# A causal FFT convolution on one core: spectrum products by 64x64 and 64x32 tiles, with the sums moved into the inverse transform

## The chip, the cores and the metric

The kernel runs on one core of a Trainium2 chip. The metric is the time of one execution on the device in microseconds (us). TensorE multiplies matrices, VectorE (DVE), ScalarE (ACT) and GpSimd (POOL) work elementwise, SyncE (SP) issues most transfers. TensorE's weights stay in its 128x128 array while the other operand streams past; a matmul can use a part of the array, a tile, given by its rows (the partitions it sums over) and columns (the partitions it writes).

## The reference

Everything is float32, S = 2048 tokens, D = 640 channels, F = 1728.

```
mod = silu(c) @ w_mod                        # six rows: sa, ca, ga, sb, cb, gb
h  = layernorm(q) * (1 + ca) + sa
ks = shift_conv(k, shift_k, 4 taps)          # causal, per channel
kv = ks * v
y  = irfft(rfft(kv, 2S) * rfft(ssm_k, 2S))[:S] + kv * ssm_D
x  = q + ga * (h * y)                        # a causal convolution of length S per channel
h2 = layernorm(x) * (1 + cb) + sb
out = x + gb * (W2 gelu(W1 layernorm(h2)^T + b1) + b2)^T      # the token-mixing MLP
```

## The kernel before

The convolution runs in five chunks of 128 channels (`for c in range(NC)`), then come the second layernorm, the first MLP product (L432) and the second (L1026 and L951). The order of instructions on each engine is the order of the code, so a chunk's stages stand one behind the other on TensorE, and the work of other engines is dealt out between them by hand (`dv(n)` issues the next n operations of the shift convolution).

A chunk's transform of 2048 tokens is split into 64 x 32. Both sides, the signal kv (in tile `x`) and the SSM kernel (permuted by `perm` on ScalarE into tile `p`), go through

- `step1` (L210), step one: a transform over 64 points for the 128 channels; two halves of 64 channels share the partitions, and the constant F1 has zeros for the other half. A matmul has 64 columns of data as weights (a 128x64 tile) and streams 128 columns. ScalarE copies the result to tile `z`.
- `f2` (L224), step two: for each of 64 frequencies k1 a 32-point transform. The constant `w2` (4 MB, tiles `w0` and `w1`) holds 128x64 weights, half of them zeros; 64 columns stream. Eight frequencies fill one PSUM buffer. Real and imaginary parts lie beside each other in a row of memory. ScalarE copies the SSM side to `kt`; VectorE multiplies the signal side with it and with its swapped copy (`mul`, two products into `p`); GpSimd forms real part minus and imaginary part plus (`add`, two sums into `y`).
- `i2` (L255), step three: the inverse over 32 points, data as weights on 32x128 tiles, real and imaginary part accumulated in PSUM.
- `i1` (L273), step four: the inverse over 64 points on 64x64 tiles; then `gate` multiplies by h and adds to x.

PSUM has a ring of three buffers for all of this. `load_ks(c + 2)` fetches the SSM kernel two chunks ahead into `aux`, from which `perm` has to read before. In the last chunk the first blocks of W1 are split into two float32r parts (`split_rows`, into `wb`), which the first MLP product uses.

Of the kernel before, what the change touches and what calls it, by code (L numbers as in the profile page):

```python
# [20 lines left out]
def _constants():  # L21


    n1, n2, k1, k2 = np.arange(64), np.arange(32), np.arange(64), np.arange(32)
# [6 lines left out]
    w2 = np.zeros((2, 32, 2, 64, 2, 2, 32))  # L31
    for c in range(2):
        w2[0, :, c, :, 0, c] = np.cos(ang)
        w2[1, :, c, :, 0, c] = -np.sin(ang)
        w2[0, :, c, :, 1, c] = np.sin(ang)
        w2[1, :, c, :, 1, c] = np.cos(ang)
    ang = 2 * np.pi * (k2[:, None] * n2[None, :] % 32) / 32
    c, s = np.cos(ang), np.sin(ang)
    v2 = np.tile(np.concatenate([c, -s, s, c], 1), (4, 1))
# [5 lines left out]
    return {"small": small.astype(np.float32), "w2": w2.reshape(128, 8192).astype(np.float32),  # L45
# [4 lines left out]
def mixer_kernel(ctx: ExitStack, tc: tile.TileContext, q, k, v, shift_k, ssm_k, ssm_D, w1, b1, w2, b2, c,  # L50
# [29 lines left out]
    T_z, T_y, T_v1 = mem("z", 8192), mem("y", 4096), mem("v", 4520)  # L80
    T_w2 = [mem("w0", 4096), mem("w1", 4096)]
# [7 lines left out]
    KSP = P.rearrange("p (i m) -> p i m", i=32)  # L89
# [7 lines left out]
    Y = T_y.rearrange("p (r i k) -> p r i k", r=2, i=32)  # L97
    W2 = [t.rearrange("p (k m) -> p k m", m=64) for t in T_w2]
# [64 lines left out]
    def perm(c):  # L163
        act.activation(KSP.rearrange("p i (n e) -> p i e n", e=2),
                       KSR.rearrange("p (e i n) -> p i e n", e=2, i=32), AF.Copy)

# [5 lines left out]
    def kv_ops(g, eng=dve):  # L172
# [8 lines left out]
        ops.append(lambda: TT(eng, X.rearrange("p (n i) -> p n i", i=64)[:, 8 * g:8 * g + 8], S_,  # L181
# [13 lines left out]
    def kv(c_next, gs=((0,), (1,), (2,), (3,))):  # L195

        ops = []
        for gl in gs:
            o = kv_ops(gl[0])

            def end(gl=gl, last=o.pop()):
                last()
                if c_next is not None:
                    for g in gl:
                        kv_loads(c_next, g)
            ops += o + [end]
        return ops


    def step1(side, t, later=False):  # L210

        ps = psum()
        for a in range(8):
            i = 8 * t + a
            lhs = KSP[:, i] if side else X.rearrange("p (m i) -> p i m", i=32)[:, i]
            o = 512 * (a % 2) + 128 * (a // 2)
            for ri in range(2):
                pe.matmul(ps[64 * ri:64 * ri + 64, o:o + 128], lhs, F1[:, 128 * ri:128 * ri + 128], start=True,  # L218
                          stop=True)
# [4 lines left out]
    def f2(g):  # L224

        ps = psum()
        for kk in range(8):
            k1 = 8 * g + kk
            for ri in range(2):
                for h in range(2):  # L230
                    o = 128 * kk + 64 * ri
                    rhs = bass.AP(tensor=T_z.tensor, offset=T_z.offset + 128 * h + 2 * k1,
                                  ap=[T_z.ap[0], [256, 32], [1, 2]])
                    pe.matmul(ps[64 * h:64 * h + 64, o:o + 64], W2[k1 // 32][:, 2 * (k1 % 32) + ri], rhs, start=True, stop=True)  # L234
        pv = ps.rearrange("p (m s i) -> p m s i", s=2, i=32)
        xs_ = pv[:, :, 0]
        kt = KT[g % 2]
        act.activation(kt.rearrange("p (m i) -> p m i", i=32), pv[:, :, 1], AF.Copy)  # L238
        pa, pb = P[:, 1024 * (g % 2):1024 * (g % 2) + 512], P[:, 1024 * (g % 2) + 512:1024 * (g % 2) + 1024]
        m16 = lambda t: t.rearrange("p (m i) -> p m i", i=32)  # L240
# [225 lines left out]
    run(kv_ops(2, pool))  # L466
    run(kv_ops(0))
    kv_loads(1, 0)
    run(kv_ops(1))
    kv_loads(1, 1)  # L470
    kv_loads(1, 2)
    run(kv_ops(3))
    sync.dma_start(T_w2[0], c_w2[:, 0:4096], max_dma_last_dim=4096)
    kv_loads(1, 3)
    sync.dma_start(T_w2[1], c_w2[:, 4096:8192], max_dma_last_dim=4096)
# [6 lines left out]
    perm(0)  # L482
    all_taps()
    load_taps(2)
    for t in range(4):
        step1(0, t)
    run(kv_ops(2, pool))
    run(kv_ops(0))
    run(kv_ops(1))
    for t in range(4):  # L490
        step1(1, t)
# [12 lines left out]
    fill = kv_ops(3)  # L504
# [6 lines left out]
    for c in range(NC):  # L511
        cn = c + 1 if c + 1 < NC else None
        ac, po = a1_ops(c)
        pend_m = pend_a = None
        for g in range(8):
            m_, a_ = f2(g)
            if pend_m:
                pend_m()
            if pend_a:
                pend_a()  # L520
            pend_a, pend_m = (pend_m and pa_next), m_
            pa_next = a_
            if c:
                for f_ in ac[2 * g:2 * g + 2]:
                    f_()
            if cn is None and g < 4:

                act.activation(X[:, 512 * g:512 * g + 1], epsc, AF.Copy)
                for b in range(2):
                    sync.dma_start(X[64 * b:64 * b + 64, 512 * g:512 * g + 512],  # L530
                                   dram(w1, (16 * b + g) * F, [[32 * F, 64], [1, 512]]))
            dv(-(-len(fill) // max((6 if c else 8) - g, 1)))
            if c and cn is not None and g == 3:
                perm_add(cn)
        pend_m()
        if pend_a:
            pend_a()
        pa_next(dve if c else pool)
# [5 lines left out]
        if c and c + 2 < NC:  # L544
            taps()
            if c + 3 < NC:
                load_taps(c + 3)
        if c == 0:
            mod_load(0, 4, P[:, 0:1920])
            for t in range(4):  # L550
                step1(0, t)
# [26 lines left out]
            run(kv_ops(2, pool))  # L578
# [5 lines left out]
            perm(1)  # L584
            load_ks(2)
            run(ac[8:16])
            run(po[0:2])
            fill.extend(kv(3, ((0,), (1, 2), (3,))))
        elif cn is not None:
            for t in range(2):  # L590
                step1(0, t)
            perm(cn)
            if c + 2 < NC:
                fill.extend(kv(c + 3 if c + 3 < NC else None))
            else:
                fill.extend(x1s(cc, j) for cc in range(c) for j in range(16))
        else:
            blk.update({f: (j16(t[:, 0:2048]), j16(t[:, 2048:4096])) for f, t in (
                (0, mem("w0", 4096, "wb0")), (1, mem("w1", 4096, "wb1")))})
# [6 lines left out]
            split_rows(0, X, (0, 1, 3))  # L606
            split_rows(1, T_aux[:, 0:2048], (0, 1, 3))
            run(po)
        if c:
            dv(7 if cn is not None else 8)  # L610
            i2(0)
            if cn is None:
                mod_part(tap, 3, pl[3])
                i2(1, dve)
                t = mem("y", 4096, "wb2")
                blk[2] = j16(t[:, 0:2048]), j16(t[:, 2048:4096])
                split_rows(0, X, (2,))
                split_rows(1, T_aux[:, 0:2048], (2,))
# [466 lines left out]
```

## Time and profile before

| | |
|---|---|
| time, median of 3 runs (lowest to highest) | 721.0 us (720.58 to 728.29) |
| the profiled execution | 722.7 us, of it a span of 720.8 us from first to last instruction |
| TensorE busy, weight loads busy | 91%, 88% of the span |
| VectorE, ScalarE, GpSimd busy | 68%, 41%, 21% |
| chunk stages; MLP | about 23 to 315 us; 315 to 721 us |
| step two in the five chunks | 42 to 67, 117 to 137, 168 to 187, 218 to 237, 269 to 288 us |

A group's row gives line, engine, operation, output and inputs by the program's names, shape and count, then busy time, the mean of one in ns, and the idle time of the engine ahead of it with what ended most of that. Names are those of tiles: `pst` is any buffer of the PSUM ring, `tap` the PSUM tile of the taps, `z` the spectrum before step two or four, `y` the product spectrum, `v` the constants, `x`, `p`, `kt`, `aux` as above. The clock in a view is the share of full speed that was granted to TensorE. The MATMUL records of a float32 matmul number two for each matmul of the program.

### The profile page before, as it was taken

To read this page: it belongs to the slowest core of one execution; us is meant where nothing else is said; L and a number is where in the kernel's file an instruction comes from. 1 tells how busy PE (TensorE), PEld (TensorE's weight loads), DVE (VectorE), ACT (ScalarE), POOL (GpSimd) and SP (SyncE) were. 2 spreads that over 40 slices of the span, in tenths; PEclk is the share of its full clock that TensorE was granted. 3 is DMA by queue.
4 is the path that set the end of the run, shared out by engine and by line. 5 is a ranking of instruction groups with operands and counts; after the bars stand their busy time and mean duration, and the time that the engine had idled before them with its cause. 6 is when DMAs were issued, how large, how long until landed. Compare 5 with 4: busy or idle time off the path is not lost.

```text
span 720.8 us, 20751 instructions
## 1 busy us (share of the span) xinstructions
PE 656.0 (91%) x9131; PEld 632.6 (88%) x9131; DVE 492.6 (68%) x861; ACT 297.4 (41%) x465; POOL 154.6 (21%) x135
## 2 busy tenths in 40 slices
PE   0797968999999999998889999999999989999997
PEld 0797758989999989777889999999999989999997
DVE  7666748969879638788894313212389768888887
ACT  0432564645745545446766223112244222333221
POOL 5187038715626328100010000000000000000000
PEclk9998889999999899879999999999999999999999
DMA  9979998527233522351203543352263423455510
GB/s 185 243 223 223 304 235 172 116 52 164 57 68 87 168 55 70 112 133 44 53 7 59 101 75 60 76 100 59 59 183 102 141 96 123 130 159 175 159 45 37
DMA packets 165903, 84.89 MB, mean 118 GB/s; under 512 B 88979, under 2 KB 157366, under 8 KB 165814
## 3 DMA queue, kind: packets, MB, share of 16 engines
q1 hardware_dynamic: 161266, 82.27, 46.1%
q10 hardware_dynamic: 4548, 1.31, 1.0%
q8 instruction: 71, 1.16, 0.7%
q14 instruction: 18, 0.15, 0.1%
HBM read 73.07 MB, written 10.49 MB: 116 GB/s over the span
## 4 chain that ended last, share of the span: by engine, by line
PE 54%; DVE 23%; ACT 6%; issue 5%; POOL 5%; DMA 4%; SPq 2%; ACTq 0%; DVEq 0%; POOLq 0%
PE pst L432 21%; PE pst L218 8%; PE pst L234 8%; PE pst L1026 7%; PE pst L263 5%; DVE m_w L59 4%; POOL y L59 4%; DVE m_x L59 3%; PE pst L282 3%; DVE tap L59 2%; ACT m_w L939 2%; PE pst L951 2%; DVE kt L59 2%; DVE m_x L960 1%; DVE m_v L59 1%
## 5 line engine op out<-in xcount | busy, mean ns | idle before, releaser
L234 PE MATMUL pst<-z,w 128*64 128x64 f32 x2560 | 96.8, 241 | 11.2 <-ACT z L220 6.1
L234 PEld LDWEIGHTS pst<-z,w 128*64 128x64 f32 x2560 | 95.4, 142 | 12.9 <-ACT z L220 7.3
L59 POOL TENSOR_TENSOR y<-p 128x256 f32<-128x256 f32 x72 | 90.6, 1315 | 27.2 <-DVE p L59 26.7
L59 DVE TENSOR_TENSOR p<-pst,kt 128x512 f32<-128x512 f32 x80 | 52.7, 688 | 29.6 <-ACT kt L238 20.9
L218 PE MATMUL pst<-v,x 128*64 128x128 f32 x640 | 48.3, 315 | 23.2 <-DVE x L59 23.2
L218 PEld LDWEIGHTS pst<-v,x 128*64 128x64 f32 x640 | 46.3, 222 | 23.7 <-POOL t L457 23.2
L220 ACT ACTIVATE z<-pst 128x1024 f32<-128x1024 f32 x40 | 45.7, 1144 | 48.9 <-PE pst L218 31.1
L238 ACT ACTIVATE kt<-pst 128x512 f32<-128x512 f32 x40 | 25.1, 628 | 58.5 <-PE pst L234 39.6
L830 ACT ACTIVATE pst<-pst,sm 128x640 f32<-128x640 f32 x14 | 10.7, 767 | 85.9 <-PE pst L432 85.9
L263 PEld LDWEIGHTS pst<-v,y 32*128 32x128 f32 x1280 | 40.5, 197 | 5.9 <-POOL y L59 2.5
L263 PE MATMUL pst<-v,y 32*128 32x64 f32 x1280 | 42.6, 283 | 2.6 <-DVE y L59 1.5
L951 PE MATMUL pst<-r_z,m_w 128*128 128x320 f32 x222 | 42.8, 312 | 2.1 <-DVE m_w L59 1.6
L218 PE MATMUL pst<-v,p 128*64 128x128 f32 x640 | 37.7, 274 | 2.4 <-issue 2.2
L939 ACT ACTIVATE m_w<-m_v 128x896 fp32r<-128x896 f32 x24 | 22.2, 949 | 42.4 <-DVE m_v L59 29.4
L218 PEld LDWEIGHTS pst<-v,p 128*64 128x64 f32 x640 | 35.2, 137 | 3.6 <-issue 3.1
L951 PEld LDWEIGHTS pst<-r_z,m_w 128*128 128x128 f32 x222 | 34.8, 188 | 3.7 <-DVE m_w L59 2.9
L59 DVE TENSOR_TENSOR tap<-tap,kt 128x512 f32<-128x512 f32 x51 | 35.5, 697 | 1.3
L59 DVE TENSOR_TENSOR kt<-in,tap 128x512 f32<-128x512 f32 x51 | 35.0, 687 | 1.4
L59 DVE TENSOR_TENSOR m_w<-m_v,m_w 128x896 fp32r<-128x896 f32 x24 | 26.0, 1087 | 10.4 <-ACT m_w L939 10.4
L271 ACT ACTIVATE z<-pst 128x512 f32<-128x512 f32 x38 | 21.2, 657 | 26.3 <-PE pst L263 26.3
L282 PEld LDWEIGHTS pst<-z,v 64*64 64x64 f32 x1280 | 23.7, 154 | 8.4 <-issue 6.3
L282 PE MATMUL pst<-z,v 64*64 64x64 f32 x1280 | 25.3, 240 | 6.1 <-DMA v<-in_const_v_dram 3.0
(277 smaller groups left out, 1425.7 us busy)
## 6 DMA issues: line engine op xcount, KB each, us to landing
x<-in_B_w_dram SPq DMA_DIRECT2D x22, 512.0 KB
m_v<-in_B_w_dram SPq DMA_DIRECT2D x15, 384.0 KB
x<-in_B_w_dram SPq DMA_DIRECT2D x14, 384.0 KB
aux<-in_A_ssm_k_dram SPq DMA_DIRECT2D x10, 512.0 KB
in<-in_A_k_dram SPq DMA_DIRECT2D x36, 128.0 KB
in<-in_A_v_dram SPq DMA_DIRECT2D x36, 128.0 KB
m_x<-xs SPq DMA_DIRECT2D x28, 160.0 KB
out_dram<-m_x SPq DMA_DIRECT2D x28, 160.0 KB
```

The lines of the kernel that those rows point to most:

```text
L59: TT = lambda eng, o, a, b, op: eng.tensor_tensor(o, a, b, op=op)
L218: pe.matmul(ps[64 * ri:64 * ri + 64, o:o + 128], lhs, F1[:, 128 * ri:128 * ri + 128], start=True, stop=True)
L220: evac = lambda: act.activation(Z[:, side, t].rearrange("p a k e -> p e a k"), ps.rearrange("p (e a k) -> p e a k", a=8, e=2), AF.Copy)
L234: pe.matmul(ps[64 * h:64 * h + 64, o:o + 64], W2[k1 // 32][:, 2 * (k1 % 32) + ri], rhs, start=True, stop=True)
L238: act.activation(kt.rearrange("p (m i) -> p m i", i=32), pv[:, :, 1], AF.Copy)
L263: pe.matmul(pp[qd // 2][:, o:o + 64], Y[p, ri, i:i + 2].rearrange("p i k -> p (i k)"), V2[p, 64 * ri:64 * ri + 64], start=ri == 0, stop=ri ...
L271: act.activation(o, i, AF.Copy)
L282: pe.matmul(ps[64 * b:64 * b + 64, 512 * e + 64 * jj:512 * e + 64 * jj + 64], V1[p, ri, n2], T2[p, :, 32 * ri + n2], start=ri == 0, stop=r ...
L432: pe.matmul(ps[0:m, h, 0:320], w_.bitcast(F32R), r_[:, 320 * h:320 * h + 320].bitcast(F32R), start=first and i == 0, stop=last and i == 2)
L939: act.activation(W[n][0].bitcast(F32R), a(w_), AF.Copy)
L951: pe.matmul(bank[n], w[:, i].bitcast(F32R), r.bitcast(F32R), start=i == 0 and k == 0, stop=i == 6 and k == 2)
L1026: pe.matmul(acc[s][:, h, 0:320], w[:, f_].bitcast(F32R), u[r + h].bitcast(F32R), start=f_ == 0 and k == 0, stop=f_ == NF - 1 and k == 2)
```

## The change

Real and imaginary parts of the spectrum now lie on partitions.

- Step one runs on 128x32 tiles: twice as many matmuls, each with 32 columns of data as weights, which now lie side by side in memory. The SSM side is read from where it was loaded, and `perm` is gone; its load for two chunks ahead moves behind step one.
- Step two has weights without zeros, 2 MB, one tile `w0`. For each frequency and each half e of the partitions one matmul on a 64x64 tile transforms both sides (128 columns); two on 64x32 tiles transform the SSM side again with its parts exchanged (64 columns each). Four frequencies fill a PSUM buffer, so there are 16 groups in place of 8.
- One VectorE product for each group gives equal products (real with real, imaginary with imaginary) and unequal ones, straight into `y`, which doubles to 8192 columns. Both GpSimd sums and the second VectorE product are gone.
- Step three sums over 64 partitions in place of 32: its constant `V2` carries the signs, and its tiles are 64x128.
- `x` and `p` hold kv of even and odd chunks, so that the next chunk's products don't wait for step one; GpSimd does a quarter of them in more chunks than before.
- With `w1` gone, W1 block 1 is split into the upper half of `y`, behind the last step three, as block 2 was before; blocks 0 and 3 stay ahead of it.

```diff
-    T_z, T_y, T_v1 = mem("z", 8192), mem("y", 4096), mem("v", 4520)
-    T_w2 = [mem("w0", 4096), mem("w1", 4096)]
+    T_z, T_y, T_v1 = mem("z", 8192), mem("y", 8192), mem("v", 4520)
+    T_w2 = mem("w0", 4096)
...
+    XK = [t.rearrange("p (i n) -> p i n", n=32) for t in (X, P)]
...
+    Y = T_y.rearrange("p (r i k) -> p r i k", r=2, i=64)
+    W2 = T_w2.rearrange("p (k m) -> p k m", m=64)
...
-    def step1(side, t, later=False):
+    def step1(cc, side, t, later=False):
...
-            lhs = KSP[:, i] if side else X.rearrange("p (m i) -> p i m", i=32)[:, i]
...
-            for ri in range(2):
-                pe.matmul(ps[64 * ri:64 * ri + 64, o:o + 128], lhs, F1[:, 128 * ri:128 * ri + 128], start=True,
-                          stop=True)
+            for e in range(2):
+                lhs = KSR[:, 32 * (32 * e + i):32 * (32 * e + i) + 32] if side else XK[cc % 2][:, 32 * e + i]
+                for ri in range(2):
+                    r = 64 * e + 32 * ri
+                    pe.matmul(ps[r:r + 32, o:o + 128], lhs, F1[:, 128 * ri:128 * ri + 128], start=True, stop=True,
+                              tile_position=(0, r))
...
-        for kk in range(8):
-            k1 = 8 * g + kk
-            for ri in range(2):
-                for h in range(2):
-                    o = 128 * kk + 64 * ri
-                    rhs = bass.AP(tensor=T_z.tensor, offset=T_z.offset + 128 * h + 2 * k1,
-                                  ap=[T_z.ap[0], [256, 32], [1, 2]])
-                    pe.matmul(ps[64 * h:64 * h + 64, o:o + 64], W2[k1 // 32][:, 2 * (k1 % 32) + ri], rhs, start=True, stop=True)
...
+        for kk in range(4):
+            k1 = 4 * g + kk
+            for e in range(2):
+                z, r = T_z[64 * e:64 * e + 64], slice(64 * e, 64 * e + 64)
+                def rhs(s_, n):
+                    return bass.AP(tensor=z.tensor, offset=z.offset + 4096 * s_ + 2 * k1, ap=[z.ap[0], [128, n], [1, 2]])
+                pe.matmul(ps[r, 0:512].rearrange("p (s k i) -> p k s i", s=2, k=4)[:, kk], W2[r, k1], rhs(0, 64), start=True,
+                          stop=True)
+                for ri in range(2):
+                    q_ = 64 * e + 32 - 32 * ri
+                    pe.matmul(ps[q_:q_ + 32, 512 + 64 * kk:576 + 64 * kk], W2[r, k1, 32 * ri:32 * ri + 32], rhs(1, 32),
+                              start=True, stop=True, tile_position=(64 * e, q_))
         kt = KT[g % 2]
-        act.activation(kt.rearrange("p (m i) -> p m i", i=32), pv[:, :, 1], AF.Copy)
+        act.activation(kt, ps[:, 256:768], AF.Copy)
...
         def mul():
-            TT(dve, m16(pa), xs_, m16(kt), ALU.mult)
-            sw = bass.AP(tensor=kt.tensor, offset=kt.offset + 32, ap=[kt.ap[0], [64, 8], [-32, 2], [1, 32]])
-            TT(dve, pb.rearrange("p (k r i) -> p k r i", k=8, r=2), xs_.rearrange("p (k r) i -> p k r i", r=2), sw,
-               ALU.mult)
-
-        def add(eng=pool):
-            for ri, t, op in ((0, pa, ALU.subtract), (1, pb, ALU.add)):
-                t = t.rearrange("p (k r i) -> p r i k", k=8, r=2)
-                TT(eng, Y[:, ri, :, 8 * g:8 * g + 8], t[:, 0], t[:, 1], op)
-        return mul, add
+            TT(dve, Y[:, :, :, 4 * g:4 * g + 4],
+               ps[:, 0:256].rearrange("p (k i) -> p i k", k=4)[:, None].to_broadcast([128, 2, 64, 4]),
+               kt.rearrange("p (r k i) -> p r i k", r=2, k=4), ALU.mult)
+        return mul
...
-                    p = slice(32 * qd, 32 * qd + 32)
-                    o, i = 512 * (qd % 2) + 64 * s, 2 * (8 * r + s)
+                    p = slice(64 * (qd % 2), 64 * (qd % 2) + 64)
+                    o, i = 512 * (qd % 2) + 64 * s, 4 * (8 * r + s) + 2 * (qd // 2)
```

How the change stands in the engines' orders: on TensorE in the first chunk, where step one of the SSM side (the input `p` before) ends and step two begins; `pst` with a number is one PSUM buffer, and the sizes are those of the output, partitions first. Before:

```order
L218 MATMUL pst_316<-v,p 64x128 x16
L218 MATMUL pst_334<-v,p 64x128 x16
L234 MATMUL pst_372<-z,w_74 64x64 x32
L234 MATMUL pst_407<-z,w_74 64x64 x32
L234 MATMUL pst_444<-z,w_74 64x64 x32
L234 MATMUL pst_483<-z,w_74 64x64 x32
L234 MATMUL pst_522<-z,w_75 64x64 x32
```

And at the same place now, where the SSM side comes from `aux`:

```order
L222 MATMUL pst_409<-v,aux 32x128 x32
L222 MATMUL pst_443<-v,aux 32x128 x32
L238 MATMUL pst_497<-z,w_74 64x2x64
L242 MATMUL pst_497<-z,w_74 32x64 x2
L238 MATMUL pst_497<-z,w_74 64x2x64
L242 MATMUL pst_497<-z,w_74 32x64 x2
L238 MATMUL pst_497<-z,w_74 64x2x64
L242 MATMUL pst_497<-z,w_74 32x64 x2
```

Where 32 matmuls of one size stood for a buffer, one of 64 output partitions and two of 32 now take turns; eight such turns fill a buffer, 128 a chunk.

On GpSimd, from the end of a shift convolution (`x<-t,in`) through the second chunk's step two (`xa` and `xb` are the two halves of the residual x, to which `gate` adds; `aux<-aux,rows` adds ssm_D). Before:

```order
L59 TENSOR_TENSOR x<-t,in 128x512
L59 TENSOR_TENSOR xa<-xa,aux 128x8x128
L59 TENSOR_TENSOR xb<-xb,aux 128x8x128
L59 TENSOR_TENSOR y<-p 128x32x8 x4
L59 TENSOR_TENSOR aux<-aux,rows 1x64 x2
L59 TENSOR_TENSOR y<-p 128x32x8 x10
```

Now:

```order
L63 TENSOR_TENSOR x<-t,in 128x8x64
L63 TENSOR_TENSOR xa<-xa,aux 128x8x128
L63 TENSOR_TENSOR xb<-xb,aux 128x8x128
L63 TENSOR_TENSOR aux<-aux,rows 1x64 x2
L537 TENSOR_SCALAR t<-rows 128x256
L63 TENSOR_TENSOR t<-in,t 128x512 x2
```

The fourteen sums into `y` are gone from this chunk, and taps and products of the shift convolution for a later chunk stand in their place.

More of the change, by code (lines that the diff above doesn't have):

```diff
@@ L513, in mixer_kernel @@
         ac, po = a1_ops(c)
[L514 to L522, printed above, removed]
+        pend = None
+        for g in range(16):
+            m_ = f2(g)
+            if pend:
+                pend()
+            pend = m_
             if c:
[L524 to L528, printed above, removed]
+                ac[g]()
+            if cn is None and g < 8 and g % 2 == 0:
+                o = 256 * g
+                act.activation(X[:, o:o + 1], epsc, AF.Copy)
                 for b in range(2):
[L530 to L533, printed above, removed]
+                    sync.dma_start(X[64 * b:64 * b + 64, o:o + 512],
+                                   dram(w1, (16 * b + g // 2) * F, [[32 * F, 64], [1, 512]]))
+            dv(-(-len(fill) // max((12 if c else 16) - g, 1)))
+            if c and cn is not None and g == 7:
                 perm_add(cn)
[L535 to L538, printed above, removed]
+        pend()
         if c == 0:
@@ L874, in t_ops @@
         rest(3, a)
[L876 removed]
+    T_wb = [mem("w0", 4096, "wb0b"), W_1]
     split_w(4)
```

113 lines of the change are left out of this document (51 added, 62 removed).

## The prediction

> **What bounds the kernel now.** I read the page's groups first, then the trace in stretches, one per channel chunk, then single places on TensorE. The two rows of one f32 matmul count: the program issues 1280 matmuls in step two and the group has 2560, so each is two records on its tile, one behind the other.
>
> ```profile
> L234 PE MATMUL pst<-z,w 128*64 128x64 f32 x2560 | 96.8, 241 | 11.2 <-ACT z L220 6.1
> L218 PE MATMUL pst<-v,x 128*64 128x128 f32 x640 | 48.3, 315 | 23.2 <-DVE x L59 23.2
> L263 PE MATMUL pst<-v,y 32*128 32x64 f32 x1280 | 42.6, 283 | 2.6 <-DVE y L59 1.5
> L218 PE MATMUL pst<-v,p 128*64 128x128 f32 x640 | 37.7, 274 | 2.4 <-issue 2.2
> ```
>
> Next, step two (L234) by chunk; columns are the stretch, its length, TensorE busy (records), weight loads busy, granted clock, DMA share, GB/s.
>
> ```profile
> 42.00:67.03 25.03, 20.08 (x512) 19.60 (x512) 0.92 0.89 217
> 117.00:136.58 19.58, 19.45 (x512) 19.06 (x512) 1.00 0.71 158
> 167.93:186.80 18.87, 18.87 (x512) 18.87 (x512) 1.00 0.56 131
> 217.68:236.54 18.86, 18.86 (x511) 18.86 (x512) 1.00 0.35 109
> 269.33:288.34 19.01, 19.01 (x512) 18.93 (x512) 1.00 0.27 74
> sum 101.35, PE 96.27 PEld 95.32; mean PE 19.25 PEld 19.06
> ```
>
> TensorE has hardly a gap in four of the five, so it is the bound of the stage that the change rewrites: 101.35 us of the 720.8. VectorE and GpSimd have slack there, and work taken from them buys little. What decides is how fast TensorE can take the new matmuls.
>
> **Step two, the first term.** For each of 64 frequencies the new order is: an equal product on a 64x64 tile with 128 columns, two unequal products on 64x32 tiles with 64 columns, then the same three for the other 64 partitions. The tile size changes four times per frequency, 256 times per chunk. Before, step two has one size throughout. So I looked at what TensorE does where the size changes (start, length, records):
>
> ```profile
> 262.09 0.62 PE L282 MATMUL pst<-z,v 64*64 64x64 f32 x29
> 262.64 0.44 PE L218 MATMUL pst<-v,p 128*64 128x128 f32 x4
> ...
> 305.73 0.85 PE L282 MATMUL pst<-z,v 64*64 64x64 f32 x23
> 306.51 0.75 PE L342 MATMUL tap<-p,sm 128*32 128x320 f32 x3
> ...
> 287.81 0.61 PE L234 MATMUL pst<-z,w 128*64 128x64 f32 x11
> 288.34 0.74 PE L342 MATMUL tap<-in,sm 128*32 128x320 f32 x6
> ...
> 236.16 0.55 PE L234 MATMUL pst<-z,w 128*64 128x64 f32 x10
> 236.54 0.32 PE L218 MATMUL pst<-v,x 128*64 128x128 f32 x1
> ```
>
> In the first three pairs the size changes. The earlier rows end, as modelled, at 262.71, 306.58 and 288.42, and the new size starts 0.07 to 0.08 us before that: the old work has left the array. The third pair changes only the width, 64 to 32, as the new step two does. In the fourth the stage changes but not the size: the start lies 0.17 us ahead of the end (236.71), and both stages' records mix. So a change of size costs nearly the whole latency of the last record; without one the latency overlaps. [...]
>
> The latencies, at both granted clocks (mean ns is the number behind the comma; clocks further below):
>
> ```profile
> L282 PE MATMUL pst<-z,v 64*64 64x64 f32 x121 | 2.0, 217 | 0.0
> L218 PE MATMUL pst<-v,p 128*64 128x128 f32 x82 | 4.6, 273 | 0.0
> L282 PE MATMUL pst<-z,v 64*64 64x64 f32 x124 | 3.6, 307 | 1.5 <-ACT wb L408 1.5
> L218 PE MATMUL pst<-v,x 128*64 128x128 f32 x28 | 3.2, 418 | 0.0
> 246.73 0.70 PE L218 MATMUL pst<-v,x 128*64 128x128 f32 x4
> ```
>
> At full clock 64 columns take 217 ns and 128 take 273, so 64 columns stream in about 0.055 us; at half clock 307 and 418, so 0.11. A 64x64 tile with 128 columns isn't in the trace; I take 270 and 415 ns. After a change of size the second record of a tile starts late: in "x4, 0.44" the second pair lasts 0.27, so it starts at 0.17; at half clock (0.70 less 0.42) at 0.28.
>
> Per frequency and half of the partitions, at half clock: equal product 0.28 + (0.415 - 0.07) = 0.625 us; the unequal pair, two tiles side by side, 0.12 (an estimate: 0.11 streaming and a little load) + (0.307 - 0.07) = 0.357. Twice their sum is 1.964 us, and 64 of them 125.7 us per chunk. At full clock: 0.17 + 0.20 and 0.085 + 0.147 give 1.20 us, 76.7 per chunk.
>
> **Which clock.** Stretches of 3.41 us, the step in which the clock changes here (columns: length, then busy of PE, PEld, DVE, ACT, POOL, granted clock, DMA share, GB/s):
>
> ```profile
> 222.00:235.00 13.00, 13.00 (x359) 13.00 (x356) 11.07 (x18) 7.47 (x16) 12.42 (x11) 1.00 0.32 95
> 240.55:243.97 3.42, 2.70 (x86) 2.47 (x86) 3.42 (x9) 3.08 (x2) 0.77 (x1) 1.00 0.02 5
> 243.97:250.79 6.82, 6.82 (x96) 6.37 (x96) 4.25 (x5) 2.52 (x5) 0.00 (x0) 0.50 0.68 154
> ...
> 291.75:295.17 3.42, 3.12 (x107) 3.02 (x105) 3.42 (x7) 1.25 (x3) 0.00 (x0) 1.00 0.76 216
> 298.58:301.99 3.41, 2.83 (x91) 2.61 (x86) 2.70 (x3) 0.73 (x2) 0.00 (x0) 1.00 0.02 5
> 301.99:308.80 6.81, 5.91 (x140) 4.11 (x140) 4.07 (x11) 1.42 (x3) 0.06 (x1) 0.50 0.01 2
> ```
>
> In 240.55 and 298.58 TensorE is busy 79% and 83%, yet 0.50 follows. Both are mostly step three, whose records fill a quarter of the array: 86 x 0.055 x 1/4 is 35% of the array's time, 91 give 37%. The stretch at 291.75 (107, 43%) is not followed by a fall, and step two now uses 359 x 0.055 x 1/2 of 13.00, 76%. So I read the clock as granted by how much of the array streams, with a limit near 0.4. The new step two streams, per frequency, four records of a quarter for 0.11 and eight of an eighth for 0.055: 0.165 us of 1.20, or 14%. I take half clock, except for some 5 us per chunk until it falls (saving 3.2 us): 122.5 us. Five are 612.5, less 101.35: **+511.2 us**. Bounds for the shorter or longer start of second records (1.81 to 2.18 us a frequency): +462 to +581.
>
> [...]
>
> **Step three (i2).** Its tiles go from 32x128 to 64x128, so two fit where four did.
>
> ```profile
> L263 PE MATMUL pst<-v,y 32*128 32x64 f32 x108 | 3.2, 270 | 0.0
> 192.54 3.22 PE L263 MATMUL pst<-v,y 32*128 32x64 f32 x108
> 204.29 2.02 PE L282 MATMUL pst<-z,v 64*64 64x64 f32 x121
> ```
>
> 107 starts in 3.22 - 0.27 are 27.6 ns apart, four tiles in 0.110 us. Step four streams as many columns, with half as wide weights, and needs only about 0.06 for four, so a tile of step three waits for its 128-wide weights. Two tiles in 0.110 make 128 records 7.0 us instead of 3.5: +3.5 for each of ten calls, one of which runs beside the load of the next weights: **+31.5**. Bounds: 0 if two tiles keep the pace of four; +62 if loading and streaming take turns in a tile (0.163).
>
> **The rest.** Behind each step two the clock stays 0.50 for one or two stretches of 3.41 us; 5 us at half speed lose 2.5, five times: **+12.5** (0 to 34, with a fall in step three). Step one doubles its records on half as wide tiles, four side by side: the same streaming. Its input side is read without stride now, and 48.3 should become the other side's 37.7; part runs at half clock: **-9** (0 to -13). TensorE's waits for the sums ahead of step three go, **-2** (0 to -5):
>
> ```profile
> PE pst L263 <- DVE y L59: 1.5, 2, 0.8
> PE pst L282 <- DMA v<-in_const_v_dram: 3.0, 1, 3.0
> PE pst L282 <- ACT wb L408: 1.5, 1, 1.5
> ```
>
> The middle row is the load named above. The last is the split of W1 blocks behind the last step three, which gets twice as long: **+1** (0 to 3).
>
> At nothing: the GpSimd sums and the ScalarE permutation go, but TensorE was not waiting for more than the rows above. The 80 products on VectorE and 80 copies on ScalarE, twice as many copies as now, lie under step two; each group of four frequencies gives them 7.7 us.
>
> ```profile
> L59 DVE TENSOR_TENSOR p<-pst,kt 128x512 f32<-128x512 f32 x80 | 52.7, 688 | 29.6 <-ACT kt L238 20.9
> L59 DVE TENSOR_TENSOR y<-p 128x256 f32<-128x256 f32 x8 | 9.3, 1205 | 0.0
> ```
>
> A product costs between 0.69 us and, written in short pieces as those sums were, 2.4; it would show only if a group took less. The constant halved to 2 MB and the later load of the SSM kernel have a whole step two of cover. Step one's input is double buffered, which lets GpSimd take a quarter of the next products in every chunk; TensorE isn't waiting for it.
>
> **The sum**, against the profiled execution (722.7 us, 1.9 around its span of 720.8; the median of the runs is 721.0): 722.7 + 511.2 + 31.5 + 12.5 - 9 - 2 + 1 = **1268 us**.
>
> **The rivals.** Second: the array drains but the clock stays full, step two 76.7 per chunk: 722.7 + 282.1 + 31.5 - 9 - 2 + 1 = **1026**. For it: gaps of 0.15 to 0.35 us are far shorter than any idle time ahead of a fall. Against: the 35% rows. Third: 64x64 and 64x32 count as one size and nothing drains. Then the two halves run beside each other, 0.33 us of streaming a frequency, 21.5 per chunk, and step three still loses: 722.7 + 6 + 31.5 - 9 - 2 + 1 = **750**. Only the pair at 288.34, one place in the run, speaks directly against it. Fourth, the other side: without a drain the weight loads of all tiles also go side by side, so step three keeps 27.6 ns and a frequency falls below 0.27 us, where VectorE's 25 operations of 0.69 (16 products, nine others) bound the stage at 17.3: 722.7 - 15 - 9 - 2 + 1 = **698**, faster. It decides from 0.35 us a frequency down, with step three at its old pace (5 x 64 x 0.35 = 112, the 101 of now and the 11 saved elsewhere); step four's pace speaks for it, every change of size against it. That the change removes less than it says I exclude: the sums are gone from GpSimd's order.
>
> **Chances.** Forecast 0.83, second 0.07, third 0.06, fourth 0.04. The forecast's terms at their bounds give 1172 to 1398; both ends together need all at once, so 1170 to 1350 holds nearly all of its 0.83, and no rival is needed to reach 0.8. Within 1%, about what a measurement here can tell from no change, 0.01; faster 0.04; slower 0.95.
>
> **What would show it.** Right: step two some 120 us per chunk, clock 0.50 in it, records of L238 and L242 never overlapping, step three near 7 us a call, VectorE idle between products. Wrong: L242's start well ahead of L238's end (third), or clock 1.00 there (second). A record with other latency than its neighbours' would move the forecast by 64 x 5 times the difference.

## The result, and the profile after

The changed kernel takes **1272.5 us** (median of 4 runs, 1264.6 to 1274.9); the kernel before, on the same chip, 720.8. The ratio is 1.760, with a 95% interval of 1.745 to 1.774. The forecast was 1268 us. The profiled execution has a span of 1262.8 us.

Step two (now L238 and L242) by chunk (columns in the first line; x is the number of instructions):

```profile
core 0: us, PE busy (x) PEld busy (x) DVE busy (x) ACT busy (x) POOL busy (x), PEclk, DMA share, GB/s
44.47:165.82 121.35, 121.35 (x772) 58.63 (x776) 20.21 (x22) 8.96 (x15) 0.00 (x0) 0.52 0.28 75
216.79:339.02 122.23, 122.23 (x772) 58.98 (x776) 27.54 (x32) 14.67 (x30) 15.36 (x13) 0.51 0.17 36
379.18:500.61 121.43, 121.43 (x772) 58.67 (x776) 17.43 (x18) 14.67 (x30) 11.89 (x11) 0.52 0.13 26
540.39:662.22 121.83, 121.83 (x772) 58.84 (x776) 17.17 (x17) 14.67 (x30) 0.70 (x2) 0.51 0.13 34
703.78:825.41 121.63, 121.63 (x771) 58.69 (x774) 22.45 (x50) 15.04 (x34) 0.00 (x0) 0.52 0.07 18
sum 608.47, PE 608.46 PEld 293.81 DVE 104.80 ACT 68.00 POOL 27.94; mean PE 121.69 PEld 58.76 DVE 20.96 ACT 13.60 POOL 5.59
```

Counted, as here, to the modelled end of the last record, the same stage took 101.8 us in five chunks and now takes 608.5: of the 542.0 us that the span grew by, 506.7 lie here. TensorE counts as busy in all of it, at a granted clock of 0.51 to 0.52. The busy share of the page (95%) would pass for a kernel that uses its engine well; the clock, and the turns shown below, say otherwise.

The costliest groups (busy us, mean ns of one, idle time ahead):

```profile
L238 PE MATMUL pst<-z,w 64*64 64x128 f32 x1280 | 429.6, 434 | 6.1 <-ACT z L224 6.1
L63 DVE TENSOR_TENSOR y<-pst,kt 128x512 f32<-128x512 f32 x80 | 83.3, 1041 | 516.1 <-ACT kt L245 516.1
L242 PE MATMUL pst<-z,w 64*32 64x64 f32 x2560 | 268.3, 305 | 0.0
L262 PE MATMUL pst<-v,y 64*128 64x64 f32 x1280 | 74.1, 273 | 0.8 <-ACT z L224 0.8
```

VectorE's product costs 1041 ns, inside the bounds of 0.69 to 2.4, and waits 516 us for its input: nothing of it shows. Now single turns on TensorE, first at full clock (1.00) at the head of the second chunk's step two, then at half clock (0.50) in the third (start, length, records):

```profile
216.79 0.43 PE L238 MATMUL pst<-z,w 64*64 64x128 f32 x2 [1.22 <-ACT z L224]
217.15 0.33 PE L242 MATMUL pst<-z,w 64*32 64x64 f32 x4
217.41 0.43 PE L238 MATMUL pst<-z,w 64*64 64x128 f32 x2
```

```profile
399.98 0.68 PE L238 MATMUL pst<-z,w 64*64 64x128 f32 x2
400.60 0.42 PE L242 MATMUL pst<-z,w 64*32 64x64 f32 x4
400.95 0.68 PE L238 MATMUL pst<-z,w 64*64 64x128 f32 x2
```

Each turn starts 0.06 to 0.07 us before the modelled end of the one ahead, as in the prediction's three pairs where the size changes. One half of one frequency takes 0.62 us at full clock and 0.97 at half: 64 x 2 x 0.62 is 79 us a chunk, 64 x 2 x 0.97 is 124.

Step three at its undisturbed pace is one row:

```profile
175.40 7.14 PE L262 MATMUL pst<-v,y 64*128 64x64 f32 x124 [0.81 <-ACT z L224]
```

### The profile page after: what moved, and what is told of

It is laid out like the page before. It is cut to its first block, busy times and chain, and to the rows that moved or that the text cites. A ratio compares the mean times of both kernels' runs of the same rounds, so it can differ in the third digit from the quotient of the medians.

```text
span 1262.8 us, 25798 instructions
## 1 busy us (share of the span) xinstructions
PE 1194.9 (95%) x11691; PEld 854.7 (68%) x11691; DVE 512.4 (41%) x837; ACT 308.6 (24%) x500; POOL 86.4 (7%) x81
## 4 chain that ended last, share of the span: by engine, by line
PE 79%; DVE 12%; ACT 4%; issue 3%; DMA 1%; SPq 0%; POOL 0%; ACTq 0%; DVEq 0%
PE pst L238 31%; PE pst L242 18%; PE pst L431 12%; PE pst L222 6%; PE pst L262 6%; PE pst L1017 4%; DVE m_x L63 2%; PE pst L942 1%; DVE m_w L63 1%; DVE y_b L63 1%; DVE aux L63 1%; PE pst L281 1%; PE tap L341 1%; DVE m_x L951 1%; DMA x<-in_B_w_dram 1%
## 5 line engine op out<-in xcount | busy, mean ns | idle before, releaser
L238 PE MATMUL pst<-z,w 64*64 64x128 f32 x1280 | 429.6, 434 | 6.1 <-ACT z L224 6.1
L63 DVE TENSOR_TENSOR y<-pst,kt 128x512 f32<-128x512 f32 x80 | 83.3, 1041 | 516.1 <-ACT kt L245 516.1
L242 PE MATMUL pst<-z,w 64*32 64x64 f32 x2560 | 268.3, 305 | 0.0
L242 PEld LDWEIGHTS pst<-z,w 64*32 64x32 f32 x2560 | 115.9, 134 | 207.1 <-issue 207.1
L238 PEld LDWEIGHTS pst<-z,w 64*64 64x64 f32 x1280 | 177.6, 196 | 114.2 <-issue 103.5
L262 PEld LDWEIGHTS pst<-v,y 64*128 64x128 f32 x1280 | 72.6, 188 | 3.7 <-issue 1.5
L262 PE MATMUL pst<-v,y 64*128 64x64 f32 x1280 | 74.1, 273 | 0.8 <-ACT z L224 0.8
L222 PE MATMUL pst<-v,aux 128*32 128x128 f32 x1280 | 39.9, 274 | 10.1 <-issue 9.7
L431 PE MATMUL pst<-r_z,y_b 128*128 128x320 f32 x252 | 40.5, 309 | 0.0
L431 PEld LDWEIGHTS pst<-r_z,y_b 128*128 128x128 f32 x252 | 37.9, 188 | 0.0
```

Source lines behind the costliest of these rows:

```text
L63: TT = lambda eng, o, a, b, op: eng.tensor_tensor(o, a, b, op=op)
L222: pe.matmul(ps[r:r + 32, o:o + 128], lhs, F1[:, 128 * ri:128 * ri + 128], start=True, stop=True, tile_position=(0, r))
L238: pe.matmul(ps[r, 0:512].rearrange("p (s k i) -> p k s i", s=2, k=4)[:, kk], W2[r, k1], rhs(0, 64), start=True, stop=True)
L242: pe.matmul(ps[q_:q_ + 32, 512 + 64 * kk:576 + 64 * kk], W2[r, k1, 32 * ri:32 * ri + 32], rhs(1, 32), start=True, stop=True, tile_position ...
L262: pe.matmul(pp[qd // 2][:, o:o + 64], Y[p, ri, i:i + 2].rearrange("p i k -> p (i k)"), V2[p, 64 * ri:64 * ri + 64], start=ri == 0, stop=ri ...
L431: pe.matmul(ps[0:m, h, 0:320], w_.bitcast(F32R), r_[:, 320 * h:320 * h + 320].bitcast(F32R), start=first and i == 0, stop=last and i == 2)
```

## The experiments

Time of step two is given per chunk at its undisturbed value. The first chunk is longer in every kernel but the changed one, before too (25.0 us). There TensorE pauses once for 3.9 us, for something that the trace doesn't name; that it is the weights' second half, whose transfer was issued 5 us ahead of the stage, is a guess. The edits are abridged, and `...` stands for what is left out.

**One size of tile (e1_one_size).** The changed kernel, its equal product cut into two 64x32 tiles too:

```diff
-                pe.matmul(ps[r, 0:512]...[:, kk], W2[r, k1], rhs(0, 64), start=True, stop=True)
+                for ri in range(2):
+                    q_ = 64 * e + 32 * ri
+                    pe.matmul(ps[q_:q_ + 32, 0:512]...[:, kk], W2[r, k1, 32 * ri:32 * ri + 32], rhs(0, 64),
+                              start=True, stop=True, tile_position=(64 * e, q_))
```

> The changed kernel with one change: the equal product too is made by two matmuls on 64x32 tiles, so step two has one tile size throughout; values, streams and weights stay. Theory (changes of tile size drain the array, and the emptied array loses its clock): no drain; two diagonal blocks stream 0.33 us a frequency, half of the array, so the clock is 1.00; step two 21 to 24 us a chunk in place of 122 (VectorE's 16 products of 1.04 us and the shift convolution need about 22), all in all 750 to 775 us. Rival (the new step two is slow by itself: more matmuls, 64-row tiles, strided operands): it gets more matmuls still and stays over 1200 us.

Measured: 830.1 us, 1.146 times before [1.138, 1.154]. Third chunk's step two:

```profile
217.61:249.58 31.97, 29.30 (x1028) 28.03 (x1032) 19.35 (x17) 14.92 (x30) 12.66 (x11) 1.00 0.50 98
```

With a third more matmuls the kernel is 442 us faster, and the clock in this chunk is 1.00: what costs is the turn of sizes, not the work. But 32 us a chunk is more than expected. The busy time of 29.3 us over 1024 records of the program is 28.6 ns a record; the expectation had counted streaming columns alone.

**Halves in turn (e7_halves_in_turn).** The same with the loop over e inside:

```diff
-            for e in range(2):             # with e1's edit
-                for ri in range(2):        # equal
...
-                for ri in range(2):        # unequal
...
+            for un in range(2):
+                for ri in range(2):
+                    for e in range(2):
...
```

> The one-size kernel (all step-two matmuls on 64x32 tiles) with its loop turned: the two partition halves alternate matmul by matmul, where one half's four came ahead of the other's four. Theory: the 9 to 10 us a chunk that the one-size kernel took beyond the forecast came from that order, since the two halves can stream side by side only when they alternate; with it the 16 records of a frequency go at the 22 ns that the grouped kernel's unequal records showed, 0.35 us, step two takes 22 to 24 us a chunk, the kernel about 785 us. Rival: what sets the pace is a price per record or per weight load whatever the order: 32 us a chunk, 830 us.

Measured: 823.9 us, 1.140 [1.133, 1.146]; 30.2 to 33.8 us a chunk. TensorE is busy for 29.0 to 29.4 us in the last four chunks, again 28.5 ns a record. The rival holds: without changes of size the order of the halves hardly matters (823.9 us for 830.1).

**Sizes grouped (e2_grouped).** The changed kernel's own matmuls, in each group of four frequencies first the 8 equal, then the 16 unequal ones; 32 changes a chunk for 256:

```diff
-        for kk in range(4):
-            for e in range(2):        # equal, then unequal
...
+        for un in range(2):           # 0 equal, 1 unequal
+            for kk in range(4):
+                for e in range(2):
...
```

> The changed kernel with step two's matmuls in another order: in each group of four frequencies first all eight equal products (64x64), then all sixteen unequal ones (64x32), so 2 changes of size a group in place of 16. Theory: equal part 7 x 0.109 + 0.05 + 0.20 = 1.01 us, unequal part 0.58, a group 1.6 us, step two about 25 us a chunk at full clock (779 us in all); the array streams 0.66 us of 1.6, 41%, just at the limit that the rows of before gave, so the clock may fall, then about 47 us a chunk and 900 us. Rival (cost goes with the matmuls, not with the changes): as the changed kernel, about 1270 us.

Measured: 806.1 us, 1.115 [1.105, 1.125]; 27.9 us in the undisturbed chunk, clock 1.00. Its turns:

```profile
216.38 1.10 PE L239 MATMUL pst<-z,w 64*64 64x128 f32 x16
217.40 0.79 PE L244 MATMUL pst<-z,w 64*32 64x64 f32 x32
218.12 1.10 PE L239 MATMUL pst<-z,w 64*64 64x128 f32 x16
```

1.74 us for four frequencies, where the theory had 1.6, and the clock is 1.00 in the last four chunks (0.91 in the first). The order of the same matmuls is worth 466 us.

**64 and 128 changes (e10_changes_64, e9_changes_128).** The grouped order over pairs of frequencies, and over single ones; e9's edit against e2's order:

```diff
-        for un in range(2):
-            for kk in range(4):
+        for kk in range(4):           # e9; e10: pairs of kk
+            for un in range(2):
...
```

> The same order over pairs of frequencies: 64 changes a chunk. Theory (92 ns a change, full clock): 0.43 + 0.09 = 0.52 us a frequency, 33 to 34 us a chunk, 832 to 835 us. Rival 1 (limit of 35 to 40%; here some 31% streams): half clock, some 52 us, 925 us. Rival 2 (0.2 us a change): 0.63 us, 40 us, 866 us.

> The changed kernel with the order of step two's matmuls turned inside a frequency: both partition halves' equal products, then both halves' unequal ones, so 128 changes of tile size a chunk (64x64 to 64x32 and back) where the changed kernel has 256 and the grouped one 32, and the halves can stream side by side. Theory: two costs beside the clock. The grouped kernel's 0.43 us a frequency is what the halves side by side take without changes; the changed kernel's 1.24 us at full clock is twice that (its halves run one behind the other) plus four changes of 92 ns. With side by side kept and two changes: 0.62 us a frequency, and if about 27% of the array streaming still holds the clock at 1.00 (the one-size kernel held it in stretches of 23 to 35%), step two takes 39 to 41 us a chunk, the kernel about 862 us. Rival 1, the prediction's limit of 35 to 40%: half clock, some 60 us a chunk, 960 to 970 us. Rival 2, nearly all of the price is the change itself (0.2 us each at full clock, twice that at half): 0.83 us a frequency at full clock, 53 us, 930 us, or at half clock above 1050 us.

Measured: e10 817.8 us, 1.137 [1.129, 1.145], 32.2 us a chunk. e9 872.8 to 894.3 us in four runs. Rows of e10 (one) and e9 (three chunks):

```profile
203.15:235.37 32.22, 32.22 (x772) 22.72 (x776) 17.91 (x18) 14.76 (x30) 12.16 (x11) 1.00 0.50 99
```

```profile
153.11:194.02 40.91, 40.91 (x772) 22.38 (x776) 27.95 (x32) 14.75 (x30) 15.69 (x13) 1.00 0.52 108
232.68:294.88 62.20, 62.20 (x772) 30.69 (x776) 17.48 (x18) 14.67 (x30) 11.94 (x11) 0.51 0.25 50
335.48:376.39 40.91, 40.91 (x772) 22.38 (x776) 17.73 (x18) 14.72 (x30) 0.69 (x2) 1.00 0.38 101
```

At full clock 32, 64 and 128 changes give 27.89, 32.22 and 40.91 us: (32.22 - 27.89)/32 is 135 ns and (40.91 - 32.22)/64 is 136 ns **a change**, and 23.6 us would be left without any. That is between the theory's 92 ns and the second rival's 200.

e9 also shows one thing that none had foreseen: the same matmuls in one execution (the longest of the four), 40.91 us at 1.00 in three chunks and 62.20 at 0.51 in another (the first chunk, 55.77 at 0.69, has both). The difference, 21.3 us, is also that between e9's fastest run and the other three (18.2 to 21.5), so those have probably one chunk more at half clock; that isn't shown.

**32 rows (e4_32_rows).** To test the reading of the clock without any change of size: the kernel before, step two reads only 32 of the 128 partitions, which leaves 96 of 128 terms of each sum out.

```diff
-                                  ap=[T_z.ap[0], [256, 32], [1, 2]])
+                                  ap=[[T_z.ap[0][0], 32], [256, 32], [1, 2]])
-                    pe.matmul(..., W2[k1 // 32][:, 2 * (k1 % 32) + ri], ...)
+                    pe.matmul(..., W2[k1 // 32][0:32, 2 * (k1 % 32) + ri], ...)
```

> The kernel before, its step two reading 32 of the 128 partitions only (32x64 tiles): 96 of 128 terms of each sum are left out. No change of size, TensorE issues as densely as before, but a quarter of the array is used. Theory (the clock goes by the share of the array that streams, limit about 0.4): 2 x 1/8 x 0.055 of 0.059 us is 23%, so 0.50 in step two, records about 54 ns apart, 27 us a chunk in place of 19, some +40 us. Rival (the clock falls only when TensorE idles): 1.00, records 30 ns apart, step two bound by GpSimd's sums at about 21 us, +10 us.

Measured: 753.6 us (one run). Third chunk's step two:

```profile
177.02:203.14 26.12, 26.12 (x514) 26.00 (x514) 16.35 (x26) 9.55 (x21) 15.60 (x16) 0.56 0.42 98
```

TensorE is busy for all 26.12 us, and the clock averages 0.56 (0.54 to 0.58 over the five chunks), where the kernel before had 1.00 in its third chunk. If it takes only the values 1.00 and 0.50, as it does in the traces of the kernel before and the changed one, that is 1.00 for about 3 us and 0.50 for the rest: an estimate, and what the theory had. Idle time isn't what takes the clock away here; the fewer rows are.

**A thin start (e11_low_start).** The grouped kernel with the changed kernel's order in the first 3 of 16 groups:

```diff
+        first = [(kk, e, un) for kk in range(4) for e in range(2) for un in range(2)]
+        grouped = [(kk, e, un) for un in range(2) for kk in range(4) for e in range(2)]
+        for kk, e, un in (first if g < 3 else grouped):
```

> The grouped kernel, with the changed kernel's order (four changes a frequency) in the first three of a chunk's 16 groups only. In the kernel with 128 changes one chunk's step two ran at full clock throughout (40.9 us) and another's at half throughout (62.2 us), with the same matmuls: the one at half clock had a thin stretch just ahead. Theory: the clock falls when little of the array streams for a stretch (some 13% in these three groups) and then stays at half, since the grouped order's share (37% of the array at full clock) is not enough to bring it back: 19 us for the three groups, then 52 frequencies at 0.8 to 0.86 us, 60 to 65 us a chunk where the grouped kernel takes 28.5, 965 to 990 us in all. Rival: the clock follows the last stretches alone and is back at 1.00 some 7 us behind the three groups, since the grouped order never lost it by itself: 45 to 47 us a chunk, about 895 us.

Measured: 885.4 us, 1.226 [1.223, 1.230], 46.3 us a chunk: the rival. The stretches of the third chunk, the thin groups, the stretch in which the clock comes back, and the rest:

```profile
239.87:260.35 20.48, 20.48 (x129) 9.95 (x128) 2.72 (x3) 1.96 (x4) 7.15 (x8) 0.50 0.70 140
260.35:263.77 3.42, 3.42 (x50) 2.59 (x53) 1.05 (x1) 0.98 (x2) 3.26 (x3) 0.50 0.00 0
263.77:284.25 20.48, 20.48 (x565) 16.93 (x560) 12.76 (x12) 11.77 (x24) 1.57 (x2) 1.00 0.02 4
```

The clock does come back: 0.50 for 3.42 us behind the thin groups, then 1.00. So the stuck chunk of e9 needs another reason. One can try the prediction's measure: 0.055 us for 64 columns at full clock, 0.11 at half, a quarter of the array for 64x64, an eighth for 64x32, hence 0.01375 us a record on average and twice that at half clock. The shares are:

| kernel | share of the array that streams | clock |
|---|---|---|
| changed kernel | 12 x 0.01375 / 1.24 = 13% at full clock | falls in every chunk |
| e4 | 512 x 0.055/8 in 19 us (the pace of before, an estimate) = 18% | falls in every chunk |
| e9 at 1.00 (40.91 us) | 768 x 0.01375 / 40.91 = 26% | stays in three chunks |
| e10, e2 | 33%, 38% | stays in the last four chunks |
| changed kernel at 0.50 | 12 x 0.0275 / 1.94 = 17% | doesn't come back |
| e9 at 0.50 (62.20 us) | 768 x 0.0275 / 62.20 = 34% | doesn't come back |
| e11 at 0.50, grouped (50 in 3.42 us) | 40% | back with the next stretch |

Within these kernels e9 lies between those that lose the clock and those that regain it, and it keeps what it enters with. The stretches in which its third chunk (which lost the clock) and its fourth (which kept it) begin:

```profile
231.05:234.46 3.41, 2.18 (x47) 1.16 (x39) 3.27 (x5) 1.08 (x1) 0.00 (x0) 1.00 0.85 162
333.45:336.86 3.41, 2.16 (x55) 1.32 (x46) 3.27 (x5) 1.40 (x2) 0.00 (x0) 1.00 0.78 158
```

TensorE was busy as long in both, so busy time doesn't decide; the first streams 17% by the measure, the second, with more of step one in it, 26%. But the measure doesn't hold as a rule. Two other stretches, e7 in its fourth chunk's step two (56 records on 64x32 tiles) and e1 in its first chunk's step three (70 records on 64x128 tiles, half of the array, the clock already at 0.50):

```profile
303.98:307.39 3.41, 1.46 (x56) 1.46 (x60) 0.56 (x1) 0.00 (x0) 0.00 (x0) 1.00 0.78 291
102.20:109.03 6.83, 6.83 (x70) 0.50 0.07 23
```

The first streams 17% with pauses and keeps 1.00 behind it; the second (length, TensorE busy, clock, DMA) streams more than half of the array and stays at 0.50 for another 3.4 us. In the kernel before, 35 and 37% were followed by a fall. So no limit on the share of the array fits all traces here, and what the clock counts stays open.

**Width alone (e3_two_sizes).** The kernel before; real columns by 128x64 as they were, imaginary ones by two 128x32 tiles, in pairs of frequencies, 64 changes a chunk:

```diff
-        for kk in range(8):
...
+        for k2 in range(4):
             for ri in range(2):
+                for kk in (2 * k2, 2 * k2 + 1):
...
+                        w = W2[k1 // 32][:, 2 * (k1 % 32) + ri]
+                        if ri == 0:
+                            pe.matmul(ps[64 * h:64 * h + 64, o:o + 64], w, rhs, start=True, stop=True)
+                            continue
+                        for q in range(2):
+                            p = 64 * h + 32 * q
+                            pe.matmul(ps[p:p + 32, o:o + 64], w[:, 32 * q:32 * q + 32], rhs, start=True, stop=True,
+                                      tile_position=(0, p))
```

> The kernel before, step two in pairs of frequencies: the real columns as now (four matmuls on 128x64 tiles), then the imaginary columns by eight matmuls on 128x32 tiles: the same values, 64 changes of width a chunk, rows unchanged. Theory: a pair takes 0.44 + 0.37 = 0.81 us in place of 0.59, step two 26 us a chunk in place of 19, +35 us in all, clock 1.00 (the array streams 55%). Rival (a change of width alone doesn't drain): 0 to +5 us.

Measured: 789.4 us, 1.093 [1.086, 1.099]; 33.3 us a chunk.

```profile
215.28 0.50 PE L237 MATMUL pst<-z,w 128*64 128x64 f32 x8
215.71 0.68 PE L241 MATMUL pst<-z,w 128*32 128x64 f32 x16
216.32 0.51 PE L237 MATMUL pst<-z,w 128*64 128x64 f32 x8
```

A change of width alone drains: each row starts 0.07 us before the end of the one ahead. The size is twice what was expected, and the surplus is in the narrow rows (0.61 us a turn where 0.37 was expected).

**All narrow (e8_all_narrow).** Its control, every product on 128x32 tiles:

```diff
+                    for q in range(2):
+                        p = 64 * h + 32 * q
+                        pe.matmul(ps[p:p + 32, o:o + 64], W2[...][..., 32 * q:32 * q + 32], rhs, ..., tile_position=(0, p))
```

> The kernel before with both the real and the imaginary columns of step two by two 128x32 tiles each: the tiles of the two-sizes kernel without any change of size, as its control. Theory: the drains made most of that kernel's +14 us a chunk; without them 1024 records of 22 to 25 ns make 23 to 26 us a chunk, 740 to 757 us. Rival: narrow tiles are slow by themselves (0.606 us for the 16 records of a pair, 38 ns each, whether a drain stands ahead or not): 39 us a chunk, about 820 us, and the drains are worth nothing at a change of width alone.

Measured: 833.1 us, 1.151 [1.145, 1.158]; 37.1 to 41.8 us a chunk. The time is the rival's, the reason isn't. The head of the fourth chunk's step two, and the groups of TensorE and ScalarE:

```profile
285.51:299.81 14.30, 11.26 (x384) 11.09 (x385) 14.13 (x9) 7.97 (x7) 0.67 (x1) 1.00 0.08 22
```

```profile
L236 PE MATMUL pst<-z,w 128*32 128x64 f32 x5120 | 157.5, 297 | 55.2 <-DVE p L59 30.3 <-issue 18.7 <-ACT z L220 6.1
L241 ACT ACTIVATE kt<-pst 128x512 f32<-128x512 f32 x40 | 117.5, 2957 | 71.8 <-PE pst L236 48.1 <-DVE p L59 23.7
L59 DVE TENSOR_TENSOR p<-pst,kt 128x512 f32<-128x512 f32 x80 | 86.5, 1199 | 36.0 <-ACT kt L241 31.4 <-POOL y L59 4.3 <-ACT aux L292 0.3
```

TensorE issues 384 records in 11.26 us (about 28.6 ns each, allowing for the last one's length) and then waits 3.04 us for VectorE. Beside these bursts ScalarE's copy takes 2957 ns for 628, VectorE's product 1199 for 688. So narrow tiles cost 28.6 ns a record by themselves, and what is on top is waiting, and in the second, third and fourth chunks a mean clock of 0.88 to 0.96. With that, e3 comes out by parts: half of 19.05 us for the wide records, 512 x 28.6 ns = 14.6 for the narrow, 64 x 0.136 = 8.7 for the changes, 32.8 of the measured 33.3.

**Step three alone (e5_step_three_64_rows).**

```diff
-                    p = slice(32 * qd, 32 * qd + 32)
+                    p = slice(64 * (qd % 2), 64 * (qd % 2) + 64)
```

> The kernel before with one edit: step three reads 64 partitions (two row groups of 64) where it read 32 (four of 32); its weights and streamed columns then come from the wrong partitions, so the values are unlike the reference's, while count and form of the matmuls are those of the changed kernel. Theory (the prediction's term): two 64x128 tiles side by side instead of four 32x128 make the ten calls 7 to 7.4 us each where they took 3.8 to 4.6, +31 us in all, 752 us. Rival: the calls grew in the changed kernel for what ran ahead of them (half clock, late sums), and here nothing changes: 721 us.

Measured: 748.7 us, 1.035 [1.029, 1.041], +26.8 us. A call in the kernel before, and the same call here:

```profile
147.12 3.98 PE L263 MATMUL pst<-v,y 32*128 32x64 f32 x128
```

```profile
151.78 7.36 PE L263 MATMUL pst<-v,y 64*128 64x64 f32 x128
```

The theory holds: 7.36 us, as long as a call of the changed kernel at clock 1.00 (186.91 to 194.27), with nothing else of the change present; in all it had +31 us, a little more than was measured.

**Input without stride alone (e6_contiguous_input).**

```diff
-        ops.append(lambda: TT(eng, X.rearrange("p (n i) -> p n i", i=64)[:, 8 * g:8 * g + 8], S_, ...
+        ops.append(lambda: TT(eng, X.rearrange("p (i n e) -> p n e i", i=32, e=2)[:, 8 * g:8 * g + 8], two(S_), ...
-            lhs = KSP[:, i] if side else X.rearrange("p (m i) -> p i m", i=32)[:, i]
+            lhs = KSP[:, i] if side else X.rearrange("p (i m) -> p i m", i=32)[:, i]
```

> The kernel before with the one part of the change that takes a stride from TensorE: the input of the long convolution is stored so that step one reads its 128x32 weights without stride; VectorE's 17 products then write with stride instead. Theory: 32 calls of step one on the input side get 0.22 to 0.28 us shorter each, 7 to 9 us in all, VectorE's writes (1.05 for 0.69 us) stay beside other work except the 2 to 2.5 us ahead of the first step two: 714 to 717 us. Rival: the weight load was hidden behind the streaming columns, and only the later start shows: 721 to 724 us.

Measured: 729.3 us, 1.008 [1.004, 1.012]: slower by 0.8%, where about 1% faster was expected. The profiled execution is the fastest of twelve, 722.4 us, as long as the kernel before's, so it can show why nothing is gained but not what the others lose. Behind the second chunk's step two:

```profile
137.22 3.71 PE L219 MATMUL pst<-v,x 128*64 128x128 f32 x64 [1.27 <-DVE p L59]
140.86 0.45 PE L264 MATMUL pst<-v,y 32*128 32x64 f32 x8
141.87 3.58 PE L264 MATMUL pst<-v,y 32*128 32x64 f32 x120 [0.56 <-DVE y L59]
```

And the group of VectorE's writes:

```profile
L59 DVE TENSOR_TENSOR x<-tap,in 128x512 f32<-128x512 f32 x17 | 19.2, 1131 | 9.0 <-PE pst L219 8.6
```

Two calls of step one take 3.71 us for 4.30, as expected, but start 1.27 us late: VectorE's writes with stride (1131 ns for 690) delay its last products, and TensorE waits for those, then for the sums behind them. VectorE isn't the bound over the span (busy for 69% of it); right behind this step two it is.

## Why the prediction was right, and where not

By its own steps, in us of the span:

| step | predicted | measured |
|---|---|---|
| step two | +511.2 | 608.5 - 101.8 = +506.7 |
| step three, ten calls | +31.5 | 74.9 - 44.2 = +30.7 |
| tails at half clock, step one, waits, split | +12.5 - 9 - 2 + 1 = +2.5 | +33.8 between the steps two, less 30.7: +3.1 |
| head of the program | 0 | +2.5 (first step two at 44.47, 42.00 before) |
| MLP | 0 | -0.9 |

- **The drain.** Right, and shown in three ways: the starts in the changed kernel (0.06 to 0.07 us before the modelled end of the turn ahead), e2 against the changed kernel (806.1 us for 1272.5), e3 for width alone (0.07 us again). It costs 135 ns a change at full clock by e2, e10 and e9.
- **Where the 102.6 us a chunk come from**, which the prediction gave as one sum: 23.6 us for the new matmuls without changes, for 19.05 (+4.5); 256 changes of 0.135 (+34.7); the two halves one behind the other, which the changes force, up to the 79.1 at full clock (+20.9, a remainder, not tried alone); the clock, 121.6 for 79.1 (+42.5).
- **The clock.** Half clock was right, and e4 shows its reason as far as it goes: fewer rows are enough, without idle time (busy for 26.12 of 26.12 us at a mean clock of 0.56). The limit was wrong: near 40% of the array by the prediction, but e10 and e2 keep 1.00 at 33 and 38%, and e9 does so in three chunks at 26%. The rows of 35 and 37% in the kernel before, on which the limit rested, have pauses of 0.6 to 0.7 us; longer ones in e7, at 17% (1.95 us of pauses in 3.41), cost no clock, so the pauses don't explain it either. That a rule which fails elsewhere gave the right clock here is in part luck: the changed kernel's 13% is the lowest share in the table. For e9 it would have meant 21 us a chunk too many.
- **The tail.** Predicted 2.5 us a chunk, measured 1.1 to 2.2: step one's first two calls behind step two take 4.8 to 5.9 us, 3.70 in the kernels at full clock.
- **Step one.** The -9 us came only in part: these two calls together take 3.70 instead of 4.31 us at full clock and the two later ones 1.95 instead of 2.31 each, -1.3 a chunk; the other side's last calls take 6.8 to 7.1 instead of 5.46, which the prediction had left at nothing (TensorE pauses in them, 0.9 us at 373.5, and the trace names no releaser). That this and the tail's error have opposite signs is luck.
- **The head.** Missed. The first step one begins 1.3 us later (24.49 for 23.19), its input side takes 1.6 us less, the other side up to step two 2.8 more, with two pauses of 0.5 and 1.7 us whose releaser the trace doesn't name. VectorE's writes with stride (1052 ns) stand behind the late start: in e6, which has them alone, step one begins 1.4 us late.
- **The third rival's 21.5 us a chunk** was too low for a kernel without drains: 23.6 by the changes' price, 29 on one size. Without drains the kernel would take, by estimate, 785 (e2's 806 less 5 x 4.3) to 830 (e1), not 750.
- **The range.** Its ends, 1172 and 1398, take the waits' term of 0 to -5 the wrong way round; by the prediction's own bounds they are 1167 and 1403. Nothing else rests on it.

## What to carry to other kernels

Before a matmul is cut into tiles of several sizes, count how often the size changes in program order, not how many multiplications are saved: here the same matmuls take 121.6 or 27.9 us by order alone. Group by size, and look at the granted clock as well: here it made 121.6 us of 79.1. No order of the new form beat the old full-size weights with their zero halves (19.05 us).

## What the hardware showed beyond that

- TensorE lost clock without a pause: in e4, with 32 rows, it is busy for all 26.12 us of the third chunk's step two at a mean clock of 0.56, where the kernel before had 1.00. And the same matmuls had 1.00 in three chunks of e9 and 0.51 in another of the same execution. Neither idle time nor the share of the array alone decides in these traces.
- On four tiles of 32 columns side by side a record started each 28.5 to 28.6 ns, on 128x32 with 64 columns (e8) as well as on 64x32 with 64 and 128 mixed (e1, e7). That isn't the shortest here: e2's 32 unequal records in 0.72 us, on tiles side by side, are 22.5 ns apart.
- In the kernel with 128x32 matmuls throughout (e8), ScalarE's copy took 4.7 and VectorE's product 1.7 times as long as before (2957 ns for 628, 1199 for 688). No run here shows why.
